# A fused attention and MoE kernel on one core: leak read from PSUM, second MoE layer by 128-token halves, and another order of the vector work in a step

## The chip, the cores and the metric

The kernel runs on one core of one Trainium2 chip. The metric is the device time of that core in microseconds (us), from the first to the last instruction, with a small start-up part on top. In what follows PE is the matrix engine (and PEld its weight loads), DVE the vector engine, ACT the scalar engine, POOL the GpSimd engine, and SPq the queue from which most transfers are issued. Every execution carries a state: a "slow" one is over 1.5% above the fastest of the same kernel.

## The reference, cut to what matters

```python
# q, k, v: (8, 8, 576, 64); tau = 0.02
scores = scale * q @ k.T
thresh = max(scores, axis=-1) - tau
scores = where(scores >= thresh, scores, -1e9)      # keep only what is within tau of the row's maximum
attn   = softmax(scores)
x      = (attn @ v)  -> (4608, 512)                  # 8 batches x 576 tokens, heads side by side
h      = x @ w_in                                    # 512 -> 2048
g      = maximum(0.01 * h, h)                        # leaky ReLU
out    = g @ w_out                                   # 2048 -> 512, fp32
```

## The kernel before

The program is one software pipeline of 144 steps. A step treats one block of 128 rows of scores for a pair of heads. PE computes the scores into PSUM (`sc`). DVE copies them out with the scale and takes the row maxima in the same instruction (`sf`, `mx`; two instructions of 0.75 us, one for each head). A tiny instruction makes `bb` = tau - maximum. ACT and POOL each add `bb` to one head's half, which gives `P`. One step later DVE clamps `P` as integers and ACT takes two exponentials into `w`, with row sums. One step after that (two after its scores) DVE takes the reciprocal of the sums and writes it beside the weights in `w`, and a DMA transposes `w` into `wt`. `LAG` = 5 steps after the scores PE multiplies `wt` by `v` (`pv`); DVE divides while it copies out (`xT`), and 128 or 256 tokens go as a group into the MoE part. That is a queue of first-layer units (`hp` in PSUM, copied by ACT to `gT`, leaked by DVE) and second-layer units (`op`, copied out as `osb`), of which each step takes about one of each.

```python
def next_h():
    if hq and not (hq[0][1] == 128 and any(n == 256 for _, n in oq)):   # narrow groups wait for bank y
        return hq.popleft()[0]
    return None

def leak():
    for G, u in leaky:
        g = G.g[u]
        nc.vector.scalar_tensor_tensor(out=g, in0=g, scalar=0.01, in1=g, op0=AX.mult, op1=AX.max)
        oq.append((lambda G=G, u=u: o_unit(G, u), G.n))
    leaky.clear()

# h_unit: one PSUM bank "h"; a 128-token group alternates "h" and "y"
hp = ps.tile([128, nj, G.n], FP32, tag="hy"[u % 2] if G.n == 128 else "h", bufs=1, name="hp")
...
nc.scalar.activation(out=G.g[u], in_=hp, func=AF.Copy, bias=0.0, scale=1.0)

# o_unit: both 128-token halves of a group side by side, in banks "o" and "y"
G.op = [ps.tile([128, 512], FP32, tag="oy"[i], bufs=1, name="op") for i in range(nh)]

for s in range(NS + LAG + 1):                 # a step
    credit = min(credit + 1.0, 2.0)           # how many units of each kind it takes
    ...
    scores(s, sc); smax(0), smax(1); bb; half of P on ACT, half of P on POOL
    ...
    # then, in this order on DVE:
    pi = max(pi, NEG)                         # clamp the previous step's P; anchor for POOL's splitting work
    reciprocal; W_ = rc                       # normalisation of the unit that is complete, then its transpose
    leak()
    for t in ptick.get(s, []): t()            # POOL splits later q and k into fp16 parts, not before the anchor
    evacs = [pv(ui) for ui in pv_at.get(s, [])]   # value product, gating
    ... second- and first-layer units of the step, gT copies ...
```

## Time and profile before

| | before |
|---|---|
| time, median of 4 runs (range) | 598.25 us (597.13 to 600.39) |
| span of the profiled run | 595.7 us |
| up to step 8 / steps 8 to 36 / 36 to 126 / 126 to 143 / tail | 50.0 / 111.4 / 336.8 / 58.2 / 39.3 us |

In the first two batches (up to step 36) nearly every unit of attention is one score block; in the next five (steps 36 to 126) it is two ("paired" steps), so steps 8 to 36 have more normalisations for their number and steps 36 to 126 more wide value products. The view of stretches gives the three middle stretches (steps 8 to 36, 36 to 126, 126 to 143), for each: start:end, length, busy time (x instructions) of PE, PEld, DVE, ACT and POOL, the PE clock, the DMA share and GB/s.

```profile
50.00:161.40 111.40, 84.96 (x1181) 58.87 (x1181) 108.70 (x279) 78.97 (x177) 63.97 (x76) 0.98 0.99 176
161.40:498.20 336.80, 284.85 (x2999) 172.91 (x2998) 314.45 (x822) 251.88 (x566) 194.35 (x210) 0.96 1.00 184
498.20:556.40 58.20, 53.42 (x592) 32.35 (x590) 56.41 (x164) 44.03 (x102) 16.59 (x17) 1.00 0.70 132
```

DVE is busy for all but 2.7 us of steps 8 to 36 and all but 22.4 of steps 36 to 126. The chain of work that ended last says the same, by engine:

```profile
DVE 53%; PE 22%; DMA 10%; ACT 7%; issue 7%; SPq 0%; DVEq 0%; POOL 0%; ACTq 0%; POOLq 0%
```

In the timeline of the kernel before (start, length, engine, line, what):

```profile
330.79 2.95 DVE L544 TENSOR_SCALAR w<-rc 128x256 f16<-128x256 f32 x1
330.95 0.75 POOL L522 TENSOR_SCALAR P<-sf,bb 128x576 f16<-128x576 f32 x1
...
332.92 0.66 POOL L148 TENSOR_SCALAR km<-km 128x576 f32<-128x576 f32 x1
```

A normalisation is booked with 2.95 us. It lies over three POOL instructions one behind the other (a `qs` part of 1.28 us at 331.67 is between the two shown). It ends at 333.74, 0.16 us after the last of these (333.58); POOL's next one starts at 333.67.

### The profile page before, as it was taken

To read this page: it belongs to the slowest core of one execution; us is meant where nothing else is said; L and a number is where in the kernel's file an instruction comes from. 1 tells how busy PE (TensorE), PEld (TensorE's weight loads), DVE (VectorE), ACT (ScalarE), POOL (GpSimd) and SP (SyncE) were. 2 spreads that over 40 slices of the span, in tenths; PEclk is the share of its full clock that TensorE was granted. 3 is DMA by queue.
4 is the path that set the end of the run, shared out by engine and by line. 5 is a ranking of instruction groups with operands and counts; after the bars stand their busy time and mean duration, and the time that the engine had idled before them with its cause. 6 is when DMAs were issued, how large, how long until landed. Compare 5 with 4: busy or idle time off the path is not lost.

```text
span 595.7 us, 14529 instructions
## 1 busy us (share of the span) xinstructions
PE 481.8 (81%) x5328; PEld 301.5 (51%) x5328; DVE 527.1 (88%) x1382; ACT 417.6 (70%) x925; POOL 294.2 (49%) x338
## 2 busy tenths in 40 slices
PE   4638779767799778877899689987899599998896
PEld 3325546545566445544555355554555355555564
DVE  5658999999999988999899799999999889999742
ACT  5657767785679677877678577786779668776632
POOL 6235852466427872478326773467536754232100
PEclk9556999999999899998999899998999989999999
DMA  8999799899899999899999999899999999657510
GB/s 209 174 192 252 131 161 181 188 225 135 173 187 170 211 184 182 172 215 181 170 214 179 175 178 149 213 203 148 196 171 212 181 162 171 126 118 147 112 54 35
DMA packets 280134, 101.86 MB, mean 171 GB/s; under 512 B 254976, under 2 KB 267264, under 8 KB 280064
## 3 DMA queue, kind: packets, MB, share of 16 engines
q1 hardware_dynamic: 267008, 92.03, 79.7%
q0 software_dynamic: 13056, 8.92, 12.1%
q8 instruction: 41, 0.67, 0.5%
q14 instruction: 29, 0.24, 0.1%
HBM read 36.70 MB, written 9.44 MB: 77 GB/s over the span
## 4 chain that ended last, share of the span: by engine, by line
DVE 53%; PE 22%; DMA 10%; ACT 7%; issue 7%; SPq 0%; DVEq 0%; POOL 0%; ACTq 0%; POOLq 0%
DVE sf L393 22%; DVE gT L222 12%; DMA wt<-w 8%; PE hp L229 7%; PE sc L333 6%; DVE w L544 6%; PE op L229 6%; DVE P L529 5%; ACT w L534 3%; DVE osb L267 3%; PE pv L364 2%; DVE xT L374 2%; ACT P L521 2%; ACT gT L243 1%; DVE bb L520 1%
## 5 line engine op out<-in xcount | busy, mean ns | idle before, releaser
L522 POOL TENSOR_SCALAR P<-sf,bb 128x576 f16<-128x576 f32 x140 | 140.1, 1001 | 245.0 <-DVE bb L520 239.8
L393 DVE TENSOR_SCALAR_CACHE_REDUCE sf<-sc 128x576 f32<-128x576 f32 x288 | 205.5, 749 | 25.7 <-PE sc L333 22.4
L521 ACT ACTIVATE P<-sf,bb 128x576 f16<-128x576 f32 x144 | 111.6, 775 | 140.0 <-DVE bb L520 139.1
L534 ACT ACTIVATE w<-P 128x576 f16<-128x576 f16 x288 | 192.4, 670 | 5.1 <-DMA wt<-w 4.7
L229 PE MATMUL op<-wout,gT 128*128 128x512 f16 x576 | 152.4, 385 | 25.8 <-DVE gT L222 19.3
L229 PE MATMUL hp<-xT,win 128*128 128x128 f16 (+1 forms) x1600 | 155.0, 247 | 18.1 <-ACT gT L243 9.8
L229 PEld LDWEIGHTS <-win 128*128 128x128 f16 x1600 | 126.2, 100 | 65.0 <-issue 30.7
L222 DVE SCALAR_TENSOR_TENSOR gT<-gT 128x512 f16<-128x512 f16 x144 | 121.6, 845 | 16.9 <-ACT gT L243 16.9
L333 PE MATMUL sc<-kst,qst 64*128 64x320 f16 (+1 forms) x1536 | 130.2, 301 | 6.3 <-DVE sf L393 4.9
L243 ACT ACTIVATE gT<-hp 128x512 f16<-128x512 f32 x144 | 83.5, 580 | 23.4 <-PE hp L229 23.4
L364 PE MATMUL pv<-wt,v 128*64 128x256 f16 (+2 forms) x1160 | 59.3, 239 | 48.3 <-DVE xT L374 26.8
L333 PEld LDWEIGHTS <-qst 64*128 64x128 f16 x1536 | 69.6, 98 | 54.2 <-issue 29.2
L229 PEld LDWEIGHTS <-gT 128*128 128x128 f16 x576 | 46.3, 98 | 86.3 <-DVE gT L222 31.5
L364 PEld LDWEIGHTS <-v 128*64 128x64 f16 x1160 | 44.0, 112 | 67.4 <-issue 58.8
L544 DVE TENSOR_SCALAR w<-rc 128x256 f16<-128x256 f32 (+1 forms) x92 | 67.6, 735 | 3.2
L529 DVE TENSOR_SCALAR P<-P 128x1152 int16<-128x1152 int16 x144 | 68.4, 475 | 0.2 <-ACT gT L243 0.2
L534 ACT ACTIVATION_READ_ACCUMULATOR w<-P 128x1 f32 x288 | 54.4, 189 | 0.0
L154 POOL TENSOR_TENSOR ks<-km,ks 128x320 f16<-128x320 f32 (+1 forms) x56 | 46.1, 842 | 1.2
L374 DVE TENSOR_TENSOR xT<-pv,wt 128x128 f16<-128x128 f32 x128 | 33.5, 295 | 5.2 <-PE pv L364 5.2
L154 POOL TENSOR_TENSOR qs<-qm,qs 128x576 f16<-128x576 f32 x28 | 35.8, 1279 | 0.0
L520 DVE TENSOR_SCALAR bb<-mx 128x2 f32<-128x2 f32 x144 | 27.3, 190 | 5.0
L116 POOL DMA_DIRECT2D v<-in_v_dram x32 | 21.3, 668 | 4.9 <-ACT qs L144 4.9
(34 smaller groups left out, 215.0 us busy)
## 6 DMA issues: line engine op xcount, KB each, us to landing
km<-in_k_dram SPq DMA_DIRECT2D x16, 576.0 KB, 4.6
qm<-in_q_dram SPq DMA_DIRECT2D x16, 576.0 KB, 4.9
out_dram<-osb SPq DMA_DIRECT2D x36, 256.0 KB, 4.1
v<-in_v_dram POOLq DMA_DIRECT2D x16, 160.0 KB, 4.4
v<-in_v_dram POOLq DMA_DIRECT2D x16, 128.0 KB, 5.4
win<-in_moe_w_in_dram POOLq DMA_DIRECT2D x8, 256.0 KB, 9.1
wout<-in_moe_w_out_dram POOLq DMA_DIRECT2D x8, 256.0 KB, 7.1
wt<-w SPq DMA_TRANSPOSE x92, 5.3
```

The source lines that it names most:

```text
L154: return nc.gpsimd.tensor_tensor(out=dst[:, h], in0=src[:, h], in1=h_[:, h], op=AX.subtract)
L222: nc.vector.scalar_tensor_tensor(out=g, in0=g, scalar=0.01, in1=g, op0=AX.mult, op1=AX.max)
L229: nc.tensor.matmul(out=out_, lhsT=lhsT, rhs=rhs, start=start, stop=stop, skip_group_check=True)
L243: nc.scalar.activation(out=G.g[u], in_=hp, func=AF.Copy, bias=0.0, scale=1.0)
L333: nc.tensor.matmul(out=sc[h][:, cols], lhsT=qt[r, g, qi, ds(2 * c, 2), :].rearrange("p t r -> p (t r)"), rhs=rhs, start=(i == 0), stop=(i ...
L364: nc.tensor.matmul(out=o_[ds(64 * h, 64)], lhsT=vt[:, pp, h, j, :], rhs=w_[:, :, 4 * h + j, :], start=(j == 0), stop=(j == 4), skip_group_ ...
L393: nc.vector.tensor_scalar(out=sf, in0=sc[h][:, ds(SC0, 576)], scalar1=C, scalar2=None, op0=AX.mult, op1=AX.max, accum_out=mx[:, h : h + 1])
L521: nc.scalar.activation(out=P_[:, 1, :], in_=sB, func=AF.Identity, bias=bb[:, 1:2], scale=1.0)
L522: (nc.vector if s < SPOOL else nc.gpsimd).tensor_scalar(out=P_[:, 0, :], in0=sa, scalar1=1.0, scalar2=bb[:, 0:1], op0=AX.mult, op1=AX.add)
L529: anchor[0] = nc.vector.tensor_scalar(out=pi, in0=pi, scalar1=NEG, scalar2=None, op0=AX.max)
L534: nc.scalar.activation(out=uW[ui][:, i, ds(576 * h, 576)], in_=P_[:, h, :], func=AF.Exp, bias=exp_bias, scale=1.0, accum_out=usm[ui][:, i, ...
L544: nc.vector.tensor_scalar(out=W_[:, :, 1152:1280].rearrange("p i (h r) -> p i h r", h=2), in0=rc[:, 0:nw, :].unsqueeze(3).to_broadcast([12 ...
```

## The change

Its intent is fourfold. (1) The leak reads `hp` from PSUM: ACT writes 0.99 x Relu(hp) and DVE adds 0.01 x hp, so that DVE has one SBUF input instead of two. (2) The second layer runs one 128-token half at a time and needs one output bank; the freed bank becomes the second one of the first layer, and the restriction in `next_h` goes. (3) In a step DVE does the leak and the MoE work first, then the normalisation, and the clamp last; POOL's splitting work hangs on the clamp and moves with it. (4) With more than 8 queued units a step earns credit for a quarter of a unit more of each layer, so that now and then a step takes two of each (a "double step"), and the last output copies are on DVE.

```diff
+    BONUS = 0.25
+    OSB_ACT = False
@@ leak, next_h
-        if hq and not (hq[0][1] == 128 and any(n == 256 for _, n in oq)):
-            return hq.popleft()[0]
-        return None
+        return hq.popleft()[0] if hq else None
-            nc.vector.scalar_tensor_tensor(out=g, in0=g, scalar=0.01, in1=g, op0=AX.mult, op1=AX.max)
+            nc.vector.scalar_tensor_tensor(
+                out=G.g[u], in0=hp, scalar=0.01, in1=G.g[u], op0=AX.mult, op1=AX.add)
... (second-layer units are queued per half, when their leaked parts are there)
@@ h_unit, o_unit
-            hp = ps.tile([128, nj, G.n], FP32, tag="hy"[u % 2] if G.n == 128 else "h", bufs=1, name="hp")
+            hp = ps.tile([128, nj, G.n], FP32, tag="h", bufs=2, name="hp")
-                nc.scalar.activation(out=G.g[u], in_=hp, func=AF.Copy, bias=0.0, scale=1.0)
+                nc.scalar.activation(out=G.g[u], in_=hp, func=AF.Relu, bias=0.0, scale=0.99)
-            G.op = [ps.tile([128, 512], FP32, tag="oy"[i], bufs=1, name="op") for i in range(nh)]
+            G.op = ps.tile([128, 512], FP32, tag="o", bufs=1, name="op")
@@ a step
-        credit = min(credit + 1.0, 2.0)
+        credit = min(credit + 1.0 + BONUS * (len(hq) + len(oq) > 8), 2.0)
+        leak()
+        evacs = [pv(ui) for ui in pv_at.get(s, [])]
+        ... first- and second-layer units (moved here) ...
         now, done = done, None
+        if now is not None:
+            ... reciprocal, normalisation, transpose (moved here) ...
         if last is not None:
             ... clamp, exponentials ...
-        ... normalisation, leak(), splitting work, MoE units (moved away) ...
+        ... POOL's splitting work, behind the clamp ...
```

More of the change, by code (lines that the diff above doesn't have):

```diff
@@ L219, in leak, with osb_act @@
     def leak():
-        for G, u in leaky:
-            g = G.g[u]
-            nc.vector.scalar_tensor_tensor(out=g, in0=g, scalar=0.01, in1=g, op0=AX.mult, op1=AX.max)
-            oq.append((lambda G=G, u=u: o_unit(G, u), G.n))
+        for G, u, hp in leaky:
+            nc.vector.scalar_tensor_tensor(
+                out=G.g[u], in0=hp, scalar=0.01, in1=G.g[u], op0=AX.mult, op1=AX.add)
+            nj = 512 // G.n
+            nv = (u + 1) * nj // 4
+            if (u + 1) * nj % 4 == 0:
+                oq.append((lambda G=G, v=nv - 1: o_unit(G, v), G.n))
+            if u == NJ // nj - 1:
+                for v in range(NJ // 4, G.n // 32):
+                    oq.append((lambda G=G, v=v: o_unit(G, v), G.n))
         leaky.clear()
     tail = [False]
+    def osb_act():
+        return OSB_ACT
     def mm(out_, lhsT, rhs, start, stop):
@@ L242, in act, with o_unit @@
                 G.g[u] = sb.tile([128, nj, G.n], FP16, tag="gT", bufs=16, name="gT")
-                nc.scalar.activation(out=G.g[u], in_=hp, func=AF.Copy, bias=0.0, scale=1.0)
-                leaky.append((G, u))
-            return act
-        return mms
-    def o_unit(G, u):
-        nj = 512 // G.n
-        nh = G.n // 128
-        if u == 0:
-            G.op = [ps.tile([128, 512], FP32, tag="oy"[i], bufs=1, name="op") for i in range(nh)]
-        for i in range(nh):
-            cols = ds(128 * i, 128)
-            for j in range(nj * u, nj * u + nj):
-                mm(G.op[i], G.g[u][:, j - nj * u, cols], w_out16[:, j, :], j == 0, j == NJ - 1)
-        if u < NJ // nj - 1:
+                nc.scalar.activation(out=G.g[u], in_=hp, func=AF.Relu, bias=0.0, scale=0.99)
+                leaky.append((G, u, hp))
+            return act
+        return mms
+    def o_unit(G, v):
+        i, v = divmod(v, NJ // 4)
+        if v == 0:
+            G.op = ps.tile([128, 512], FP32, tag="o", bufs=1, name="op")
+        op = G.op
+        for j in range(4 * v, 4 * v + 4):
+            nj = 512 // G.n
+            mm(op, G.g[j // nj][:, j % nj, ds(128 * i, 128)], w_out16[:, j, :], j == 0, j == NJ - 1)
+        if v < NJ // 4 - 1:
             return None
-        ops = G.op
         def fin():
-            osbs = []
-            for i, op in enumerate(ops):
-                osb = sb.tile([128, 512], FP32, tag="osb", bufs=3, name="osb")
-                if i == 1 or not tail[0]:
-                    nc.vector.tensor_copy(out=osb, in_=op)
-                else:
-                    nc.scalar.activation(out=osb, in_=op, func=AF.Copy, bias=0.0, scale=1.0)
-                osbs.append(osb)
-            def store():
-                for i, osb in enumerate(osbs):
-                    nc.sync.dma_start(out=G.rows[i], in_=osb)
-            return store
+            osb = sb.tile([128, 512], FP32, tag="osb", bufs=3, name="osb")
+            if osb_act():
+                nc.scalar.activation(out=osb, in_=op, func=AF.Copy, bias=0.0, scale=1.0)
+            else:
+                nc.vector.tensor_copy(out=osb, in_=op)
+            return lambda: nc.sync.dma_start(out=G.rows[i], in_=osb)
         return fin
@@ L419 @@
     SCS = [[(0, 9, f"sc{i}", 1, 16)] for i in range(2)]
-    HYS = [[(0, 5, "h", 1, 8), (5, 4, "y", 1, 8)]] * 2
+    HS = [[(0, 5, "h", 2, 8), (5, 4, "h", 2, 8)], [(0, 5, "o", 1, 8), (5, 4, "pv", 1, 8)]]
     def lo_all(nm, hb):
@@ L447, in second @@
         for i in range(2):
-            turn_pe("k", 0, 1, i, HYS[i], "act")
+            turn_pe("k", 0, 1, i, HS[i], "act")
     def third():
         for i in range(2):
-            turn_pe("q", 0, 1, i, HYS[i], "act" if i else "dve")
+            turn_pe("q", 0, 1, i, HS[i], "act" if i else "dve")
     at(0, second)
@@ L524 @@
             prev = (P_,) + unit_of[s]
-        now, done = done, None
+        leak()
+        evacs = [pv(ui) for ui in pv_at.get(s, [])]
+        for i in range(max(len(ou), len(hu))):
+            if i > 0:
+                leak()
+            o = ou[i]() if i < len(ou) else None
+            h = hu[i]() if i < len(hu) else None
+            if i == 0:
+                for f in evacs:
+                    f()
+                evacs = []
+            for f in (h, o):
+                if f:
+                    g_ = f()
+                    if callable(g_):
+                        stores.append(g_)
+        for f in evacs:
+            f()
+        now, done = done, None
+        if now is not None:
+            nw = size[now]
+            rc = sb.tile([128, 2, 2], FP32, tag="rc", bufs=3, name="rc")
+            nc.vector.reciprocal(out=rc[:, 0:nw, :], in_=usm[now][:, 0:nw, :])
+            W_ = uW[now][:, 0:nw, :]
+            nc.vector.tensor_scalar(
+                out=W_[:, :, 1152:1280].rearrange("p i (h r) -> p i h r", h=2),
+                in0=rc[:, 0:nw, :].unsqueeze(3).to_broadcast([128, nw, 2, 64]), scalar1=1.0, scalar2=None, op0=AX.mult)
+            uwt[now] = sb.tile([128, 2, 10, 128], FP16, tag="wt", bufs=NWT, name="wt")
+            nc.sync.dma_start(
+                out=uwt[now][:, 0:nw].rearrange("p i j r -> p (i j) r"), in_=W_.rearrange("p i c -> p (i c)"),
+                transpose=True)
         if last is not None:
@@ L538 @@
                 done = ui
-        if now is not None:
-            nw = size[now]
-            rc = sb.tile([128, 2, 2], FP32, tag="rc", bufs=3, name="rc")
-            nc.vector.reciprocal(out=rc[:, 0:nw, :], in_=usm[now][:, 0:nw, :])
-            W_ = uW[now][:, 0:nw, :]
-            nc.vector.tensor_scalar(
-                out=W_[:, :, 1152:1280].rearrange("p i (h r) -> p i h r", h=2),
-                in0=rc[:, 0:nw, :].unsqueeze(3).to_broadcast([128, nw, 2, 64]), scalar1=1.0, scalar2=None, op0=AX.mult)
-            uwt[now] = sb.tile([128, 2, 10, 128], FP16, tag="wt", bufs=NWT, name="wt")
-            nc.sync.dma_start(
-                out=uwt[now][:, 0:nw].rearrange("p i j r -> p (i j) r"), in_=W_.rearrange("p i c -> p (i c)"),
-                transpose=True)
-        leak()
         for t in ptick.get(s, []):
             t()
-        evacs = [pv(ui) for ui in pv_at.get(s, [])]
-        for i in range(max(len(ou), len(hu))):
-            o = ou[i]() if i < len(ou) else None
-            if i > 0:
-                leak()
-            h = hu[i]() if i < len(hu) else None
-            if i == 0:
-                for f in evacs:
-                    f()
-                evacs = []
-            for f in (h, o):
-                if f:
-                    g_ = f()
-                    if callable(g_):
-                        stores.append(g_)
-        for f in evacs:
-            f()
         for t in tick.get(s, []):
```

## The prediction

> **What bounds the kernel now.** I read, in this order, the busy shares, the groups by shape, single lines' spread of durations, the timeline of a few steps, and the waits. A "step" below is one score block; there are 144, and each writes `bb` once, so the starts of `bb` in the timeline are the clock of the steps: step 8 at 50.0 us, step 36 at 161.4, step 126 at 498.2, step 143 at 556.4, end at 595.7.
>
> ```profile
> PE 481.8 (81%) x5328; PEld 301.5 (51%) x5328; DVE 527.1 (88%) x1382; ACT 417.6 (70%) x925; POOL 294.2 (49%) x338
> ```
>
> The vector engine (DVE) is the busiest. From 50.0 to 556.4 its busy time is 479.6 of 506.4 us in the view of stretches, so in the loop it is nearly always occupied. The groups say with what (columns: line, engine, operation, count, then busy us and mean ns):
>
> ```profile
> L393 DVE TENSOR_SCALAR_CACHE_REDUCE sf<-sc 128x576 f32<-128x576 f32 x288 | 205.5, 749 | 25.7 <-PE sc L333 22.4 <-PE sc L339 2.4
> ...
> L222 DVE SCALAR_TENSOR_TENSOR gT<-gT 128x512 f16<-128x512 f16 x144 | 121.6, 845 | 16.9 <-ACT gT L243 16.9
> ...
> L544 DVE TENSOR_SCALAR w<-rc 128x256 f16<-128x256 f32 x52 | 44.6, 858 | 1.8
> ...
> L544 DVE TENSOR_SCALAR w<-rc 128x128 f16<-128x128 f32 x40 | 23.0, 575 | 1.4
> ```
>
> Busy is not the same as working. The spread of two lines (min/median/max ns) shows it:
>
> ```profile
> L222 DVE SCALAR_TENSOR_TENSOR gT<-gT x144: 671/684/1805, 57.5 to 589.6; 128x512 f16<-128x512 f16 x144
> ```
> ```profile
> L520 DVE TENSOR_SCALAR bb<-mx x144: 169/170/660, 13.9 to 556.4; 128x2 f32<-128x2 f32 x144
> ```
>
> The leak (L222) needs 684 ns but takes up to 1805. 144 x 0.684 = 98.5 us against 121.6: **23 us of the leak is waiting, booked as busy.** The timeline shows for whom (start, length, engine; one clean step):
>
> ```profile
> 302.05 0.17 DVE L520 TENSOR_SCALAR bb<-mx 128x2 f32<-128x2 f32 x1
> 302.13 0.46 DVE L529 TENSOR_SCALAR P<-P 128x1152 int16<-128x1152 int16 x1
> ...
> 302.41 0.79 POOL L522 TENSOR_SCALAR P<-sf,bb 128x576 f16<-128x576 f32 x1 [1.70 <-DVE bb L520]
> 302.50 0.17 DVE L542 RECIPROCAL rc<-sm 128x4 f32<-128x4 f32 x1
> 302.71 0.64 DVE L544 TENSOR_SCALAR w<-rc 128x256 f16<-128x256 f32 x1
> ```
>
> The normalisation (L544) begins inside the GpSimd (POOL) operation, which ends at 303.20, and ends 0.15 us after it. In the last steps, where POOL has nothing, the 128-column form takes 0.23 us instead of 0.58. Around 127.62 a leak of 1.80 us lies over a POOL subtraction of 1.27. So DVE and POOL shut each other out, and that is the removable part of the DVE bound.
>
> The second bound is PE order. Of the waits, two lines matter for the change (us, times, longest):
>
> ```profile
> PE op L229 <- DVE gT L222: 19.3, 20, 2.6
> ...
> PE hp L229 <- DVE osb L267: 8.0, 3, 3.3
> ```
>
> In the 3.3 us case a first-layer unit stood in bank "y" behind the output copy, PE then ran slowly, and the maxima at 342.18 started 3.50 us late: a step of 7.94 us. A second step of 7.94 us follows at 472.1.
>
> **What the Trainium skill says.** (1) "SBUF — State Buffer", section "Who interferes with whom": a DVE instruction with two SBUF inputs contends with a GpSimd one that reads SBUF; one with at most one SBUF input outside the two-port modes does not; plain `tensor_scalar` may take a two-port mode; the later of the two blocks fully. The trace agrees (0.23 against 0.58, 0.684 against 1.80). (2) "VectorE: DVE Perf Modes", section "The TRN2 errata — SBUF-src ops pay a fixed extra latency per instruction": a one-per-cycle fp32 two-input add takes (N+151)/0.96 ns, 691 for N=512. The trace has 684 for the leak and 681 for a 512-column copy out of PSUM. (3) "PSUM — Partial Sum Buffer", section "Specifications (TRN2)": eight banks of 512 fp32. Scores take four, and h, o, y, pv one each; the change makes that h twice, o and pv. (4) "ScalarE: Activation LUTs", section "Table sets: the hidden batching unit": relu and copy are in every table set. So Relu for Copy should cost nothing: 577 ns stays, and the one table load stays one; no run before the change can show this.
>
> **The change part by part.**
>
> *Leak from PSUM.* Same 144 instructions, now one input in PSUM. By the 681 ns copy and 296 ns for the 128-column product from PSUM, which scales to 296 + 384/0.96 = 696, I take 0.69 us: +1 us in all, and the 23 us of waiting go from this line.
>
> *Order in a step.* Before: `bb`, clamp, normalise, leak, gating, copy. After: `bb`, leak, gating, copy, normalise, clamp. POOL's own half of P runs from 0.36 to 1.15 us after `bb`. The port-free leak (0.60 from start to next start) now fills this time. In a one-block step (batches 0 and 1, most of the last) the gating adds 0.2 and the reciprocal 0.2, so the normalisation starts near 1.1 and waits hardly at all: 3.41 us (the commonest step in batches 0 and 1) less 0.3 is 3.1. In the paired steps the two clean forms are now 3.28 (with a normalisation, no gating) and 3.15 (gating, no normalisation); the first falls by some 0.15, the second not at all. With 0.15 us per step for output copies this is 3.37 before and 3.29 after.
>
> *What comes back.* POOL's splitting work waits for the clamp. It will start at the end of the step, 1.2 us before the next `bb` (0.68 and 0.80 from start to start of the two maxima, less about 0.2 for the signal and the overlap), and `bb` itself is a plain tensor_scalar that POOL can shut out (660 ns above; nine cases over 0.29 now). POOL's chains, from the timeline: scaling 0.67, q part 1.28, k parts 1.42 together. A step with scaling and k parts has 2.1, so `bb` waits 0.9; the step with q, scaling and k parts has 3.4. Over the steps of one batch this adds to 6 us if nothing slips into a gap, against 11.3 (L544: 40.1 less 45 x 0.64 in the view of stretches) + 10.4 (leak: 69.3 less 86 x 0.684) + about 2 us in the five batches between steps 36 and 126 now, so 4.7 a batch. I take 4.5 after: **in the paired batches contention moves rather than goes.**
>
> *PE.* Two banks for h and none shared with outputs removes both 7.94 us steps (2 x 4.6 = 9 us). Second-layer units use a leak made a step earlier in DVE order, so the 19 us of PE waits mostly go. Against that: one bank for outputs (a copy before each of 36 groups' successors), and nine steps with two units of each kind by the code's queues, where DVE waits for a fresh Relu (estimate 0.5 us each, 4 us).
>
> *Sum by stretch.* Up to 50.0: unchanged. Steps 8 to 36 (111.4 us): 28 x 3.25 (3.1 plus copies) = 91, plus 8 contention and 3 idle: 102, saves 9. Steps 36 to 126 (336.8): 90 x 3.29 = 296, plus 5 x 4.5 = 22 contention, plus 6 PE and transpose waits (over 17 now), 4 double steps: 328, saves 9; I take 11 since shut-out time overlaps PE waits. Steps 126 to 143: 17 x 0.25, saves 4. Tail of 39.3 us: no stall on the shared bank (1.4) and second-layer units left over at the end instead of a unit-by-unit chain, saves 2 to 3. Total **about 26 us: 572.**
>
> **The rivals.** *PE becomes the bound.* From the timeline: scores 0.83, second layer 0.88, first layer 0.97, value product 0.67 every second step: 3.02 us a step at full clock, against 3.29 for DVE. For it: PE at 81%, and copies before an output bank will add holes. Against: PE may be about a microsecond late in a step before DVE notices, because scores are ready before the maxima. It would leave some 10 us of the gain: 585.
>
> *The transpose loop takes over.* The normalised weights go out by a DMA (median 5.3 us to land, up to 8.6 in the loop) and are needed three steps later. Normalisation moves back 0.3 to 1 us in the step and steps get shorter, so the value product will wait oftener; it already waits 12.0 us, 14 times, in the loop. If each of the 45 paired units held PE 0.5 us more and DVE felt half, this costs 11 us: 583.
>
> *POOL contention really goes.* If `bb` and clamp slip between POOL's instructions, all 23 us of the leak and half of L544's 40 us over its own need (67.6 less 52 x 0.3 and 40 x 0.23, 0.3 an estimate) go: 43 us and the 9 of PE: 546 to 555.
>
> *It loses.* A longer chain clamp, exponentials, sums, normalisation stalls ACT and DVE. By my times the exponentials end 0.6 us before the reciprocal, so this is unlikely.
>
> **Range and chances.** 572, between the first two rivals (583, 585) and the third (about 552). Range 555 to 588. Two per cent is 586.0: chances 0.76 faster, 0.21 same, 0.03 slower.
>
> **What would show it.** Right: L222 with median near 0.69 and maximum near it; L544 means near 0.4; no first-layer wait on output copies; Relu at 577 ns; no step of 7.9 us. Also right: `bb` and clamp gain some 15 to 25 us over their medians. If `bb` stays at 0.17 throughout, the return was overstated and the time is below 560. If the maxima wait for scores by more than 20 us in the loop, PE or the transpose took over, and the waits before the value product say which.

## The result, and the profile after

The changed kernel took 580.17 us (median of 4, 578.35 to 582.82), the kernel before 598.25 on the same chip. The ratio is 0.9697, with a 95% interval of 0.9649 to 0.9746: 3.0% faster. (Ratios here and below are the mean time of one kernel's fast runs over the mean of the other's in the same rounds, so they are not quite the ratio of the medians that are quoted.) The predicted time was 572 in a range of 555 to 588.

The busy line of the page, for the kernel after:

```profile
PE 487.7 (84%) x5328; PEld 308.7 (53%) x5328; DVE 480.6 (83%) x1385; ACT 427.4 (74%) x922; POOL 251.8 (44%) x338
```

DVE lost 46.5 us of busy time (527.1 to 480.6), but the run only 18. DVE is no longer the busiest engine. The stretches of the kernel after, cut at the same steps (same columns as before), tell where:

```profile
47.10:148.40 101.30, 87.42 (x1165) 59.48 (x1164) 92.74 (x280) 81.56 (x179) 58.49 (x76) 0.94 1.06 189
148.40:478.70 330.30, 286.82 (x3012) 178.62 (x3012) 287.12 (x823) 260.58 (x570) 160.93 (x210) 0.96 1.02 188
478.70:536.90 58.20, 54.87 (x599) 33.34 (x597) 53.20 (x163) 45.50 (x103) 13.01 (x17) 1.00 0.75 136
```

In the paired steps DVE's busy time fell by 27.3 us (314.45 to 287.12), but its idle time rose from 22.4 to 43.2, so the stretch is only 6.5 us shorter. POOL's busy time fell by 33 us as well, with as many instructions: its waits for DVE had been booked as work too (its half of `P` takes 760 ns in the mean instead of 1001, see below). The chain that ended last has changed hands in part:

```profile
DVE 38%; DMA 27%; PE 23%; ACT 7%; issue 3%; SPq 0%; ACTq 0%
```

By line, the DMA's share of the chain on the transposes `wt<-w` was 8.5% before and is 25.9% now. The groups of the kernel after (line, engine, operation, count, busy us and mean ns, idle before):

```profile
L394 DVE TENSOR_SCALAR_CACHE_REDUCE sf<-sc 128x576 f32<-128x576 f32 x288 | 205.7, 750 | 37.8 <-PE sc L334 30.0 <-PE sc L340 7.6
...
L523 POOL TENSOR_SCALAR P<-sf,bb 128x576 f16<-128x576 f32 x140 | 106.5, 760 | 217.7 <-DVE bb L521 213.9 <-DVE rc L548 2.4
L221 DVE SCALAR_TENSOR_TENSOR gT<-hp,gT 128x512 f16<-128x512 f32 x144 | 98.5, 684 | 18.8 <-ACT gT L253 18.6
...
L521 DVE TENSOR_SCALAR bb<-mx 128x2 f32<-128x2 f32 x144 | 35.2, 245 | 5.0
```

The leak has gone from a mean of 845 ns to its own 684 (its longest is now 693, not 1805), and POOL's half of `P` from 1001 to 760. The normalisation, taken by its wide shape, fell from 858:

```profile
L550 DVE TENSOR_SCALAR w<-rc 128x256 f16<-128x256 f32 x52 | 21.0, 404 | 1.8
```

Of the instructions that POOL can hold up only `bb` got dearer in sum, from 27.3 us (190 ns each, at most 660) to 35.2 (at most 1801). A clean paired step of the kernel after in the timeline:

```profile
227.25 0.17 DVE L521 TENSOR_SCALAR bb<-mx 128x2 f32<-128x2 f32 x1
...
227.32 0.69 DVE L221 SCALAR_TENSOR_TENSOR gT<-hp,gT 128x512 f16<-128x512 f32 x1
...
227.61 0.75 POOL L523 TENSOR_SCALAR P<-sf,bb 128x576 f16<-128x576 f32 x1 [2.17 <-DVE bb L521]
227.92 0.17 DVE L548 RECIPROCAL rc<-sm 128x4 f32<-128x4 f32 x1
228.13 0.38 DVE L550 TENSOR_SCALAR w<-rc 128x256 f16<-128x256 f32 x1
...
230.25 0.17 DVE L521 TENSOR_SCALAR bb<-mx 128x2 f32<-128x2 f32 x1
```

POOL's half of `P` (227.61 to 228.36) now begins beside the leak, and neither is longer for it (0.69 and 0.75 us). The normalisation follows at 228.13, of 0.38 us, and the next `bb` comes at 230.25, 3.00 us after this one. The step before, without a normalisation, took 2.91. The kernel before had 3.28 for the first kind and, with no splitting work beside it, 3.01 for the second (2.93 to 3.15 in most of those where POOL also begins other work).

The idle time is in the waits (engine, tile and line waiting, for what: us in total, times, longest). Before:

```profile
PE pv L364 <- DMA wt<-w: 20.0, 16, 7.2
...
PEld L364 <- DMA wt<-w: 8.4, 2, 7.6
```

After:

```profile
PE pv L365 <- DMA wt<-w: 53.2, 32, 5.9
...
DVE sf L394 <- PE sc L334: 30.0, 26, 4.1
PEld L365 <- DMA wt<-w: 19.4, 10, 6.4
```

Inside the loop alone (from step 8 to 143) the value product's waits for the transposed weights rose from 12.7 to 53.3 us, and DVE's waits for scores from 18.2 to 33.9. One such case in the timeline of the kernel after:

```profile
203.79 0.29 DVE L550 TENSOR_SCALAR w<-rc 128x256 f16<-128x256 f32 x1
...
207.16 7.48 SPq L554 DMA_TRANSPOSE wt<-w  x2
...
213.63 1.28 PE L365 MATMUL pv<-wt,v 128*64 128x256 f16 x10 [2.61 <-DMA wt<-w]
...
214.84 1.89 PE L239 MATMUL op<-wout,gT 128*128 128x512 f16 x4
...
219.86 0.76 DVE L394 TENSOR_SCALAR_CACHE_REDUCE sf<-sc 128x576 f32<-128x576 f32 x1 [4.05 <-PE sc L334]
```

The normalisation was written by 204.1, but its transpose left the queue only at 207.16, behind transposes of `q` (201.35) and `k` (204.29). (The line merges two transposes; the second belongs to the next unit.) The product that needs it waited 2.61 us and began at 213.63. The scores behind it in PE's order were late too, and more than the wait: the granted PE clock was 0.50 in the view of stretches from 213 to 219 us, and the product took 1.28 us instead of 0.74, the four second-layer products 1.89 instead of 1.04. So the maxima waited 4.05 us at 219.86, and that step took 8.25 us. The clock was at half for 27.3 us of steps 36 to 126 in this run, for 23.9 in the kernel before.

### The profile page after: what moved, and what is told of

Same layout as the page of the kernel before. It is cut to its first block, busy times and chain, and to the rows that moved or that the text cites. A ratio compares the mean times of both kernels' runs of the same rounds, so it can differ in the third digit from the quotient of the medians.

```text
span 577.4 us, 14379 instructions
## 1 busy us (share of the span) xinstructions
PE 487.7 (84%) x5328; PEld 308.7 (53%) x5328; DVE 480.6 (83%) x1385; ACT 427.4 (74%) x922; POOL 251.8 (44%) x338
## 4 chain that ended last, share of the span: by engine, by line
DVE 38%; DMA 27%; PE 23%; ACT 7%; issue 3%; SPq 0%; ACTq 0%
DMA wt<-w 26%; DVE sf L394 16%; PE op L239 8%; DVE gT L221 7%; PE hp L239 7%; DVE P L560 4%; ACT w L565 4%; PE sc L334 4%; DVE w L550 4%; PE pv L365 4%; DVE osb L275 3%; DVE xT L375 2%; DVE bb L521 1%; DMA qm<-in_q_dram 1%; DVE rc L548 1%
## 5 line engine op out<-in xcount | busy, mean ns | idle before, releaser
L523 POOL TENSOR_SCALAR P<-sf,bb 128x576 f16<-128x576 f32 x140 | 106.5, 760 | 217.7 <-DVE bb L521 213.9
L334 PE MATMUL sc<-kst,qst 64*128 64x320 f16 (+1 forms) x1536 | 136.2, 298 | 17.1 <-DVE sf L394 13.8
L522 ACT ACTIVATE P<-sf,bb 128x576 f16<-128x576 f32 x144 | 111.3, 773 | 44.5 <-DVE bb L521 41.4
L221 DVE SCALAR_TENSOR_TENSOR gT<-hp,gT 128x512 f16<-128x512 f32 x144 | 98.5, 684 | 18.8 <-ACT gT L253 18.6
L334 PEld LDWEIGHTS <-qst 64*128 64x128 f16 x1536 | 73.7, 97 | 69.3 <-issue 44.2
L365 PE MATMUL pv<-wt,v 128*64 128x256 f16 (+2 forms) x1160 | 61.9, 246 | 57.5 <-DMA wt<-w 53.2
L157 POOL TENSOR_TENSOR ks<-km,ks 128x320 f16<-128x320 f32 (+1 forms) x56 | 40.4, 742 | 9.4 <-DVE P L560 8.2
L521 DVE TENSOR_SCALAR bb<-mx 128x2 f32<-128x2 f32 x144 | 35.2, 245 | 5.0
L550 DVE TENSOR_SCALAR w<-rc 128x256 f16<-128x256 f32 (+1 forms) x92 | 34.3, 373 | 3.2
L275 DVE COPY osb<-op 128x512 f32<-128x512 f32 x36 | 24.5, 682 | 7.5 <-PE op L239 7.5
```

The lines of the kernel that those rows point to most:

```text
L157: return nc.gpsimd.tensor_tensor(out=dst[:, h], in0=src[:, h], in1=h_[:, h], op=AX.subtract)
L221: nc.vector.scalar_tensor_tensor(out=G.g[u], in0=hp, scalar=0.01, in1=G.g[u], op0=AX.mult, op1=AX.add)
L334: nc.tensor.matmul(out=sc[h][:, cols], lhsT=qt[r, g, qi, ds(2 * c, 2), :].rearrange("p t r -> p (t r)"), rhs=rhs, start=(i == 0), stop=(i ...
L365: nc.tensor.matmul(out=o_[ds(64 * h, 64)], lhsT=vt[:, pp, h, j, :], rhs=w_[:, :, 4 * h + j, :], start=(j == 0), stop=(j == 4), skip_group_ ...
L522: nc.scalar.activation(out=P_[:, 1, :], in_=sB, func=AF.Identity, bias=bb[:, 1:2], scale=1.0)
L523: (nc.vector if s < SPOOL else nc.gpsimd).tensor_scalar(out=P_[:, 0, :], in0=sa, scalar1=1.0, scalar2=bb[:, 0:1], op0=AX.mult, op1=AX.add)
```

## The experiments

All ran with three timing rounds (four timed runs each), beside the kernel before on the same chip; its medians in the three sessions were 598.62, 599.99 and 599.41. The third session (the fifth buffer alone, and the later product with other edits) was on another chip than the first two, so times across it are compared to within a few us only. All gave correct results. Theory A: the reorder and the PSUM leak freed DVE nearly as the third rival had it, but steps got so short that the transpose, due three steps after its normalisation, became the wait that ends steps. Theory B: the transposes only absorb time that another bound (contention on `bb` and the clamp, or PE itself) would have taken anyway.

**One more step for the transposes.** In the changed kernel the value products of all but the first batch and the last four units come one step later; a fifth `wt` buffer makes room.

```diff
-    NWT = 4
+    NWT = 5
-        pv_at.setdefault(EARLY.get(ui, last + LAG), []).append(ui)
+        late = 0 < units[ui][0] and ui < len(units) - 4
+        pv_at.setdefault(last + LAG + late, []).append(ui)
```

> The changed kernel with the value product one step later (six steps after the last score block of a unit in place of five, from the second batch on, except the last four units) and five transposed-weight buffers in place of four. Theory A (the gain of DVE was given back because the value product waits for transposed weights that land too late): PE waits on the transposes fall from 72.6 us to below 30, DVE idle before the maxima from 37.8 us to below 20, time falls by 8 to 16 us to 564 to 572. Rival B (PE itself, at about 3.0 us of matmuls a step, is the bound): the waits on transposes fall as well, but the maxima wait for scores as before and the time stays within 4 us of 580.

Measured: 563.19 us (562.22 to 565.67), ratio 0.944 (0.9403 to 0.9477), 17 us under the changed kernel and a little more than expected. From its waits:

```profile
PE pv L365 <- DMA wt<-w: 24.2, 14, 5.7
```

In the whole run the waits for `wt` fell from 72.6 to 34.5 us (expected: below 30), in the loop from 53.3 to 17.9 (13.7 + 4.2), and DVE's waits for scores there from 33.9 to 12.2. DVE is the busiest engine again (485.7 us, 87%). Theory A holds: the transposes did end steps. With the waits most of PE's half clock went too: it held for 6.8 us of steps 36 to 126, against 27.3. As a control, the buffer alone:

> Control for the later value product: the changed kernel with five transposed-weight buffers in place of four and the value product where it was. Theory A says the landing comes late, not that a buffer is missing: within 3 us of 580, PE waits on the transposes still above 60 us. If the fifth buffer was what helped, about 565.

The fifth buffer without the later product gave 576.16 and 581.24 us in its two fast runs (584.81 and 588.76 count as slow), ratio 0.9661 (0.9596 to 0.9725), with waits of 52.3 + 19.6 us like the changed kernel's. It is the step that helps, not the buffer.

**The same on the kernel before.** The same edit.

> The kernel before with the same later value product and five buffers. Theory A: in the kernel before the transposes cost little (12.7 us of PE waits in the loop), so it gains less than 5 us: 593 to 598. If it gains as much as the changed kernel does, the transposes were a bound all along and theory A does not explain what was given back.

Measured: 603.95 us, ratio 1.011 (1.0072 to 1.0147): 1.1% slower, where a small gain had been expected. Its waits for `wt` fell to 8.4 + 7.8 us, but the tail grew from 39.3 to 43.1 us and first-layer waits on output copies from 8.0 to 14.6. So the later product is worth nothing to the kernel before; it pays in the changed kernel, where DVE has been freed. That is what A says and more than I had expected of it.

**The leak from SBUF again**, in the changed kernel with all else kept.

```diff
-                out=G.g[u], in0=hp, scalar=0.01, in1=G.g[u], op0=AX.mult, op1=AX.add)
+                out=G.g[u], in0=G.g[u], scalar=0.01, in1=G.g[u], op0=AX.mult, op1=AX.max)
-                nc.scalar.activation(out=G.g[u], in_=hp, func=AF.Relu, bias=0.0, scale=0.99)
+                nc.scalar.activation(out=G.g[u], in_=hp, func=AF.Copy, bias=0.0, scale=1.0)
```

> The changed kernel with the old leak: plain copy on ACT, leak from SBUF with two SBUF inputs, everything else changed. In the new order the leak stands right behind bb, where POOL starts its half of P. If the PSUM input is what frees DVE from POOL, the leak rises from 684 to 800 to 1000 ns mean, or POOL's P does from 760 to above 950, and the time rises by 5 to 15 us to 585 to 595. If the order alone does it, the leak stays near 690 and the time within 3 us of 580.

Measured: 589.13 us, ratio 0.9866 (0.9824 to 0.9907), 9 us above the changed kernel. In its groups the leak is at 724 ns and, as the clearer sign, POOL waits again:

```profile
L523 POOL TENSOR_SCALAR P<-sf,bb 128x576 f16<-128x576 f32 x140 | 134.9, 964 | 205.6 <-DVE bb L521 201.9 <-DVE rc L548 2.4
```

DVE's busy time went up by 20 us, to 500.6, for 9 us of time. Only 5.8 us of that are the leak's; the normalisation got 10.5 us dearer and the clamp 5.4. That fits a POOL that waits for the leak, ends later, and then lies over what follows on DVE.

**The old order in a step**, with PSUM leak, banks and credit kept: clamp, normalisation, leak and POOL's splitting work stand before the MoE units, as they did.

```diff
+        now, done = done, None
+        ... clamp, exponentials; reciprocal, normalisation, transpose ...
         leak()
+        for t in ptick.get(s, []):
+            t()
         evacs = [pv(ui) for ui in pv_at.get(s, [])]
...
-        ... the same, behind the MoE units ...
```

> The changed kernel with clamp, normalisation and POOL's splitting work back in front of the first and second layer, as in the kernel before. The normalisation meets POOL's P again: w near 0.64 and 0.58 us in place of 0.40 and 0.33, some 25 us more of DVE busy time, and bb back at 190 ns mean (8 us less). Prediction's view: 7 to 14 us slower than the changed kernel, 587 to 594. Theory A's extra: the transposes are issued no later than before, so PE waits on them fall to near 30 us, which gives part back; if A outweighs contention the time is 575 to 582.

Measured: 590.74 us, ratio 0.9888 (0.9834 to 0.9943), 10.6 us above the changed kernel. Its groups by shape show the contention back on the normalisation, and `bb` undisturbed at 183 ns:

```profile
L545 DVE TENSOR_SCALAR w<-rc 128x256 f16<-128x256 f32 x52 | 43.9, 844 | 1.8
```

DVE's busy time is 504.6 us. The waits for `wt` are 36.1 + 12.1 us, more than I had expected (near 30): the transposes are due as early as ever, and steps are shorter than in the kernel before. So each of the two parts, with the other in place, is worth some 20 to 24 us of DVE time, and 9 to 11 us of the run.

**PSUM leak and new order without the new banks**, on the kernel before: one bank for a wide `hp`, now held until the leak has read it.

```diff
-            nc.vector.scalar_tensor_tensor(out=g, in0=g, scalar=0.01, in1=g, op0=AX.mult, op1=AX.max)
+            nc.vector.scalar_tensor_tensor(out=g, in0=hp, scalar=0.01, in1=g, op0=AX.mult, op1=AX.add)
-                nc.scalar.activation(out=G.g[u], in_=hp, func=AF.Copy, bias=0.0, scale=1.0)
+                nc.scalar.activation(out=G.g[u], in_=hp, func=AF.Relu, bias=0.0, scale=0.99)
... (and the new order in a step; banks, queues and credit as before)
```

> The kernel before with the leak from PSUM and the new order in a step, but with the old banks and the second layer for a whole group: what the change would be without the half-at-a-time part. A first-layer bank is then held until the leak of the next step, and 256-token groups have one. PE waits of the first layer on the leak should appear (tens of us). If two banks are what makes the PSUM leak worth having, the time is above 590, perhaps above 598; if DVE contention alone matters, it is within 5 us of 580.

Measured: 637.31 us, ratio 1.0624 (1.059 to 1.0658). Its waits:

```profile
PE hp L229 <- DVE gT L222: 83.6, 81, 2.3
```

Paired steps took 4.2 us in the median (3.28 in the changed kernel), and DVE waited 110 us for scores. The second bank is what makes the PSUM leak pay: `hp` stays in its bank until DVE's leak has read it, so with one bank for wide units 81 first-layer units stood behind the leak of the one before. (New order and PSUM leak were not run one by one with the old banks.)

**`bb` on ACT**, so that POOL cannot shut it out.

```diff
-            nc.vector.tensor_scalar(out=bb, in0=mx, scalar1=-1.0, scalar2=tau_f, op0=AX.mult, op1=AX.add)
+            nc.scalar.activation(out=bb, in_=mx, func=AF.Identity, bias=tau_t, scale=-1.0)
```

> The changed kernel with bb computed on ACT (Identity, scale -1, bias tau) instead of DVE: the DVE instruction that POOL's splitting work now shuts out is taken away, and nothing else. DVE loses 35.2 us of busy time, of which 10.8 are shut-out over the median. If the shut-out of bb is what the change paid most for, the time falls by 6 to 12 us to 568 to 574. If DVE time is no longer what ends a step (theory A: the transposes do), DVE idle time grows by nearly as much and the time stays within 4 us of 580; the shut-out may also move on to the clamp.

Measured: fast runs at 576.24, 576.71 and 581.28 us, ratio 0.9635 (0.9584 to 0.9687). The fourth, at 615.37 (clock 0.742), was the one profiled, so its profile is not read. The time is within 4 us of the changed kernel and the intervals overlap, so contention on `bb` is not what the change paid most for. The same edit beside the later products:

> The later value product with bb on ACT. Once the transposes no longer end the steps, DVE time should count again: bb takes 33.7 us there, 9 of them shut out. If so the time falls by 5 to 12 us from 563 to 551 to 558. If PE is the bound by then (86 per cent busy), or the shut-out only moves to the clamp (79.0 us there against 68.1), it stays within 3 us of 563.

Measured: 552.87 us (549.72 to 557.66), ratio 0.9237 (0.9179 to 0.9294): 10 us under the version with later products alone. DVE's busy time falls from 485.7 to 463.4 us. So DVE's time counts again once the late transposes are out of the way. The edit takes all of `bb` off DVE, 33.7 us, of which 9.2 were over its median; how much of the 10 us is contention and how much its own work was not separated.

**Transposes of q and k one step later**, to see whether `wt` is late because it stands in the queue behind them.

```diff
-                    at(t0 + i + (g or 0), lambda nm=nm, b=b, hb=hb, g=g: turn(nm, b, hb, g))
+                    at(t0 + i + (g or 0) + 1, lambda nm=nm, b=b, hb=hb, g=g: turn(nm, b, hb, g))
```

> The changed kernel with every DMA transpose of split keys and queries issued one step later, so that the queue of DMA issues does not stand before one whose data POOL has not finished, with the transposed weights behind it. If that standing is why weights land late (theory A's first half: issue delays of up to 6 us, 0.8 us mean in the paired batches), PE waits on them fall from 72.6 to about 45 us and the time by 4 to 9 us. If the transfer itself or the later normalisation is the cause, waits stay over 60 us and the time within 3 us of 580.

Measured: 587.13 us, ratio 0.9799 (0.9762 to 0.9836), slower: a miss. The waits for `wt` fell, from 72.6 to 61.7 us in the whole run, and the mean delay from normalisation to issue from 0.79 to 0.55 us. But score products of the early batches now waited 9.3 + 10.1 us for their own transposed `q`, so the total is no clean test. Steps 36 to 126 have none of that, and took 328.5 us against 330.3. The fifth buffer alone, with the schedule of the changed kernel, took 325.1 there, so 1.8 us is no difference. That standing in the queue matters is not shown; if it does, it is a small part.

**No extra credit.**

```diff
-    BONUS = 0.25
+    BONUS = 0.0
```

> The changed kernel without the extra unit credit: no step has two units of each layer. The prediction put 0.5 us of DVE waiting on each of the nine double steps, 4 us; the trace has waits of 0.5 to 1.4 us of the leak for a fresh Relu at six of them. But the units that the credit pulled forward are then left for the tail, about nine pairs at 1.76 us of PE each, 16 us, less the nine double steps' own PE time. Expected 4 to 14 us slower, 584 to 594; if the double steps cost as much as the tail, the same.

Measured: 574.01 us (three fast runs, 571.47 to 574.35, and one at 584.63 that counts as slow), ratio 0.9553 (0.9516 to 0.9591): some 6 us faster, where I had expected it slower. The tail is 41.4 us against 40.6, so the credit shortens the tail by next to nothing. By the code's queues it takes only two first-layer units out of the tail (7 left instead of 9). Steps 126 to 143, with two of the double steps, take 54.8 us without it, 58.2 with it; steps 36 to 126, with six, take 324.8 and 330.3. Beside the later products:

> The later value product (563 us) without the extra unit credit. By the queues the credit takes only two first-layer units out of the tail, 1.8 us of PE, and costs waits of the leak for a fresh Relu (20.5 us of such waits with the later value product, tail included) and doubled PE steps. Without it the changed kernel was 6 us faster; here I expect 3 to 7 us, so 556 to 560.

Measured: 555.73 us (553.77 to 560.13), ratio 0.9292 (0.9234 to 0.9349): 7.5 us faster, at the edge of what was expected. And all three together:

> All three together: later value product, no extra credit, bb on ACT. If the gains add, 546 to 555; the bound would then be PE with about 3.0 us a step.

Measured: 552.7 us (550.84 to 555.9), ratio 0.9232 (0.9191 to 0.9274). That is inside the expected range, but no better than without touching the credit. The two gains (7.5 and 10 us alone) do not add. At that point PE is busy 87% of the span and DVE 84%; what bounds this version was not settled. It is 7.7% faster than the kernel before and 4.7% faster than the changed kernel.

## Why the prediction was right and wrong

The time was in the range and the direction right, but that the total is so near is luck: two terms of the sum were off in opposite directions, more contention gone than predicted and a larger cost of late transposes.

**What held.** The leak's median is 684 ns (predicted 0.69 us), with its longest at 693; all 23.1 us of waiting left that line. Relu takes a median of 578 ns, Copy took 577, and there is still one table load. First-layer waits on output copies are gone. The sign for the second rival came as well: the maxima waited 33.9 us for scores in the loop (over 20), and the value product's waits say that it was the transpose. Steps 8 to 36 lost 10.1 us (9 predicted). Steps 36 to 126 lost 6.5 instead of 11; steps 126 to 143 lost nothing instead of 4; the tail grew by 1.2 instead of shrinking by 2 to 3. The part up to step 8 gave 2.9 us where none was expected, but over the runs here it varies from 46.7 to 51.1, so nothing is read into it.

**The step that failed: "in the paired batches contention moves rather than goes".** The sum had 22 us of contention left in the five paired batches, 4.5 a batch. Over their medians `bb` now has 6.9 us there and the clamp 2.5, 9.4 together (4.1 before), and the normalisation, 18.5 us for 45, has none left over the 0.64 us each that the prediction counted as its need. In the whole run they were to gain 15 to 25 us over their medians and are at some 14 (10.7 for `bb`, 35.2 less 144 x 0.170, and 3.3 for the clamp), of which 5 were there before. What left is far more: 23 us from the leak and 33.3 from the normalisation (67.6 to 34.3). The third rival's 43 us were nearly right for DVE: 23.1 + 33.3 less 8 for what came back is 48.

The timelines show where it went. All of the leak's waiting was against POOL's splitting work: the 37 leaks that lay over it took 1.2 to 1.5 us in the mean, the others, POOL's `P` beside them or not, 0.68 (there POOL waited, not DVE: the `P` at 299.40 took 1.31 us beside a leak of 0.69). Of the 45 normalisations of the paired steps 25 lay over splitting work, at 1.09 us in the mean; in the kernel after 3 do. The splitting work now starts at the end of a step, and 62 of its 96 us in the paired steps lie over the two maxima (52 of 102 before), which have one input, in PSUM, and take 0.75 us before and after. That it starts there the prediction had. But it let `bb` wait 0.9 us and more behind a chain, if nothing slips into a gap, and the 32 `bb` that lie over splitting work take 0.39 us in the mean, 0.22 more than alone. The clean steps gained more than predicted, too ("the first falls by some 0.15, the second not at all"): 0.28 with a normalisation (3.28 to 3.00) and 0.10 without (3.01 to 2.91; the prediction's 3.15 is the time of steps in which POOL has more to do). Undoing the order brings 844 ns back to the normalisation; undoing the PSUM leak brings 964 ns back to POOL.

**The other one: transposes.** The sum had 6 us of PE and transpose waits in the paired batches, and the second rival put its cost at 11. The loop's waits for `wt` came to 53.3 us and cost 15 to 17 us of time, which is what one more step of slack gave back (580.2 to 563.2 by the medians). The rival was right and too small, and its mechanism was half wrong. The normalisation is not later in the step: it ends 1.59 us after `bb` begins in the mean of the paired units, 1.62 before. The steps are shorter. A product is due three steps after its normalisation; with two clean steps at 5.91 us instead of 6.29, three are 0.6 us shorter (3/2 x 0.38). On top, the mean delay to issue rose from 0.49 to 0.79 us and the mean landing from 6.04 to 6.27 (the prediction's 5.3 is the median of all transposes, the half-size ones of single blocks included). Counted unit by unit in the paired steps, PE came to the product 7.04 us after the end of the normalisation in the median before and 6.29 after, while `wt` landed 6.33 and 6.89 us after it: 13 of 45 were late before, 22 after. A schedule counted in steps loses real time when steps get faster; that is the term that the prediction did not have. Nor did it have the half clock that came with the longest of these waits.

**Two steps of 7.94 us.** They went, as predicted, with the shared bank. But steps of 8.45, 8.25 and 7.14 us came in, each behind a late transpose and with PE at half clock, so the predicted 9 us did not show in the total. The bank mattered more than the prediction had it, in another way: without it, PSUM leak and new order cost 6.2%.

**The credit and double steps.** These were put at 0.5 us for each of nine steps, 4 us in all, with a gain of 2 to 3 in the tail. They cost about 6, and the tail repaid at most 0.8. In one such step the leak waited 1.39 us for its Relu (262.18) and the step took 4.87; the eight in the loop took 4.3 to 6.0. The share in the last 17 steps is 3.4 us. Steps 36 to 126 are 5.5 us shorter without the credit, but they were 5.2 shorter too in the run with the fifth buffer, which has the credit; so where the rest falls stays open.

**Left open.** Why issue and landing became 0.2 to 0.3 us slower was not tested by itself. The DMA engines are busy all through the paired steps (share 1.00 before, 1.02 after), so their load is a candidate; but the fast version with `bb` on ACT moves the same bytes at 202 GB/s there, against 188, so their throughput was not the bound of the changed kernel. A kernel with the banks alone, and neither PSUM leak nor new order, was not run; so the worth of the banks by themselves is not known. PE as the bound (the first rival) was not seen in the changed kernel, but it is not excluded in the fastest version.

## What to carry to other kernels

An engine's busy time can hide waiting: compare each line's mean with its shortest, and see what lies beside the long ones before you count on its work. When you free the busiest engine, work out anew every deadline that is counted in steps, because a transfer of fixed length has less time in shorter steps; here one more step of slack was worth nearly as much as the whole change. And look at what a change needs as well as at what it gains: without the second bank, PSUM leak and new order together lose 6%.

## What the Trainium skill lacked or had wrong

- "SBUF — State Buffer", section "Who interferes with whom": the rule itself agreed (the leak's longest fell from 1805 to 693 ns with one input in PSUM, and POOL's half of `P` from 1001 to 760 ns in the mean). What is missing is what a blocked instruction does when the other engine has several in a row. Both happen here: one normalisation was held for 2.95 us over three POOL instructions, while the leak at 127.62 (1.80 us) ended 0.55 us after the first of two, and the second then took 1.11 us instead of 0.67. The page also does not say that the profile books this waiting as the instruction's own duration, which is part of why DVE looked 88% busy.
- "VectorE: DVE Perf Modes", section "The TRN2 errata — SBUF-src ops pay a fixed extra latency per instruction": its table gives a PSUM source 62 cycles more than an SBUF one (the section itself says that the SBUF row is too low). For a two-input instruction with one input in PSUM it has no row, and here the surcharge is absent: the leak took a median of 684 ns with both inputs in SBUF and 684 with one in PSUM. The section's formula for the two-input add, (N+151)/0.96 = 691 ns, is within about 1% of both.
- "DMA: Bandwidth & Descriptors", section "Latency and other measured facts": it has a bandwidth for DMA transposes (261 GB/s, by which a 655 KB `wt` would be an estimated 2.5 us), but no time from issue to landing. Here that was 5.3 us in the median of all 92, 3.3 to 13.0, and 5.9 for the 655 KB ones of the paired steps, and it is what the schedule had to allow for.
